# Nine single identity products in two banks instead of four double ones in one, and a new order of all operations

## The chip, the cores and the metric

The kernel runs on one core of a Trainium2 chip. The metric is the time of one execution on the device in microseconds (us), and of several executions the median. The core's engines are TensorE (PE in the profile; its weight loads have a row of their own, PEld), VectorE (DVE), ScalarE (ACT), GpSimd (POOL) and SyncE (SP), which here issues nearly all DMA transfers, in order.

## The reference

There is a linear attention over 8 batches, 8 heads, 576 rows and 64 columns, followed by a feed-forward network (FFN) over the 4608 resulting rows:

```python
q_s = softmax(q, axis=d)          # 64 columns
k_s = softmax(k, axis=s)          # 576 rows
kv  = einsum('bhsd,bhse->bhde', k_s, v)
x   = einsum('bhsd,bhde->bhse', q_s, kv)  -> (4608, 512)
h   = x @ w_in                    # 512 -> 2048
g   = h if h >= 1, 0 if h <= -1, else (h + 1)**2 / 4
out = g @ w_out                   # 2048 -> 512
```

Inputs and outputs are 32-bit floats.

## The kernel before

The 4608 rows are nine chunks of 512 rows. The hidden 2048 columns are sixteen blocks of 128. Each 32-bit operand of the FFN is split into a high and a low part, so that one product of 128x128 by 128x512 is three matmuls (high by low, high by high, low by high).

Chunks 0 to 2 are plain: for each block the first layer (`first_layer`, its matmuls are on line 1496, out is the bank h), then `middle`, which forms g on ACT (relu, line 1666), ACT or POOL (square, lines 1670 and 1672) and DVE (line 1676), then the split of g into its high part on ACT (line 1718) and its low part on DVE (line 1722), then the second layer (line 1733, into four banks o). Chunks 3 to 8 are taken in three pairs, in which two by two blocks of the FFN's matrices are multiplied with seven products instead of eight: the first-layer products are on line 1560 (banks hA, hb, hC), the second-layer ones on line 1876 (banks yA, yB, yC). Weights for these are formed in the plain chunks, stored to device memory (tiles b, s, r) and fetched back as tiles w and w_y (line 650 for the first layer's).

The attention of each chunk runs beside the FFN of an earlier one. The attention of the first chunk stands alone in the head of the program: for each of four head pairs a kt tile (line 996 loads it) has its maximum taken on DVE (nm, line 1013), its exponential on ACT (line 1017), and is transposed on TensorE into the banks ep and et (lines 1024 and 1027); q has its maximum, exponential and sum taken (line 1078), is divided by the sum on POOL (line 1069, with DVE's lines 1082 and 1084 before it) and transposed into tp (line 1089); then kv (line 1042) and x (line 916). In later chunks (`attention_two`) kt is loaded only for its maximum; the maxima go to device memory and come back as a tile m that holds them along the columns (lines 1252 and 1260), k is loaded, has m subtracted on DVE (line 1269) and its exponential taken on ACT (line 1275), and goes into kv (line 1285).

What TensorE does before the first ep is products of the identity matrix with itself, whose results nobody reads. Nine of them (`more_warm`, line 2189) are issued ahead of everything, into the bank o3. `keep_warm` adds operations to the plan that do the same (line 2055); it is called once, for four operations in the bank a.

All operations of all engines are first collected in a list and numbered (`Plan.op`). Then `Plan.settle` puts them in order: SEQUENCE is a written table of all the numbers, and it is the order in which the operations are emitted, and so the order of each engine and of SP's loads and stores; it is asserted that each operation stands behind those that it depends on. SECOND is a table of those operations that go to their second choice of engine. A ring hands out the rooms of a buffer in this order, so the tables also decide which room a tile gets, and which earlier reader it must wait for.

Of the kernel before, what the change touches and what calls it, by code (L numbers as in the profile page):

```python
# [99 lines left out]
class Ring:  # L100
# [330 lines left out]
def tile_linear_attention_then_ffn(  # L431
# [1617 lines left out]
    def keep_warm(pool, tag, n, due):  # L2049

        def again_(i):
            def emit():
                t = pool.tile([P, P], F32, tag=tag, name=f"warm_{tag}_{i}")
                for _ in range(2):
                    nc.tensor.matmul(t, ident, ident, start=True, stop=True)
# [205 lines left out]
```

## Time and profile before

| what | value |
|---|---|
| median of 3 runs | 796.65 us (796.65, 797.94, 794.04) |
| the profiled execution's own time | 800.3 us |
| its span | 798.5 us |
| mean granted TensorE clock | 0.995 |
| PE busy | 783.1 us (98%) |
| DVE, ACT, POOL busy | 591.2, 480.5, 410.8 us |

The span reaches from the first to the last instruction of the core. A matmul's end is modelled in the profile and matmuls are pipelined, so busy time is not time at the peak rate. An idle time is shown in brackets before the instruction that ends it, with the instruction on another engine, or the transfer, that released it.

### The profile page before, as it was taken

The page shows a single profiled execution, that of the slowest core. Times are in us where ns is not written, and L with a number is a line of the kernel's source. Part 1 is how long each engine was busy: PE and PEld are TensorE (multiplying, and loading weights), DVE is VectorE, ACT ScalarE, POOL GpSimd, SP SyncE. Part 2 cuts the span into 40 slices and gives each one's busy share as a digit, 9 for nine tenths or more (in the row PEclk, how much of TensorE's full clock was granted, in tenths as well). Part 3 has the DMA queues.
Part 4 walks back from the last instruction along what each step waited for, and adds up shares of the span by engine and source line. Part 5 has one row for each costly group of instructions (what it writes and reads, how often), then busy time and mean ns, then how long its engine had stood idle before and what let it go on. Part 6 is the DMA issues. An engine that isn't in the chain of part 4 may idle for free.

```text
span 798.5 us, 12268 instructions
## 1 busy us (share of the span) xinstructions
PE 783.1 (98%) x4134; PEld 630.7 (79%) x4134; DVE 591.2 (74%) x996; ACT 480.5 (60%) x895; POOL 410.8 (51%) x355
## 2 busy tenths in 40 slices
PE   7999999999989999999999999999999999999998
PEld 6787888877767778777777888777878888888886
DVE  6988876667757788788878975768897746577942
ACT  6978765544455666565666655676755635556551
POOL 5655676656554645355451564435713444356344
PEclk8999999999999999999999999999999999999999
DMA  8898997989898988888767767666656666666664
GB/s 310 294 294 278 306 340 264 298 269 303 294 316 275 328 279 292 286 288 276 245 192 269 238 234 252 203 222 211 211 184 213 216 205 215 186 206 212 211 210 133
DMA packets 76463, 200.75 MB, mean 251 GB/s; under 512 B 8688, under 2 KB 16880, under 8 KB 76400
## 3 DMA queue, kind: packets, MB, share of 16 engines
q1 hardware_dynamic: 76256, 199.84, 75.4%
q8 instruction: 33, 0.54, 0.3%
q14 instruction: 30, 0.25, 0.1%
q10 hardware_dynamic: 144, 0.13, 0.0%
HBM read 159.02 MB, written 40.91 MB: 250 GB/s over the span
## 4 chain that ended last, share of the span: by engine, by line
PE 75%; DMA 10%; DVE 5%; ACT 3%; POOL 3%; issue 2%; SPq 2%; ACTq 0%; DVEq 0%; POOLq 0%
PE hA L1560 16%; PE yA L1876 16%; PE o L1733 9%; PE hC L1560 8%; PE h L1496 7%; PE yC L1876 7%; PE hb L1560 4%; PE yB L1876 3%; DMA m<-mk 2%; PE x L916 2%; PE kv L1285 1%; DMA mk<-mt 1%; DMA w_y<-r 1%; DMA s<-w_s 1%; DVE k L1269 1%
## 5 line engine op out<-in xcount | busy, mean ns | idle before, releaser
L1852 ACT CAST y<-B 128x512 fp32r<-128x512 f32 x160 | 98.9, 621 | 79.0 <-PE yA L1876 33.1
L1560 PE MATMUL hA<-x,w 128*128 128x512 f32 x576 | 142.2, 391 | 0.9 <-ACT yo L477 0.5
L1856 POOL TENSOR_TENSOR y<-B,y 128x512 fp32r<-128x512 f32 x57 | 79.1, 1390 | 107.2 <-ACT y L1852 107.0
L1560 PEld LDWEIGHTS hA<-x,w 128*128 128x128 f32 x576 | 107.4, 188 | 25.9 <-issue 1.0
L1876 PE MATMUL yA<-y,w_y 128*128 128x512 f32 x528 | 125.1, 390 | 0.0
L1733 PE MATMUL o<-wh,g 128*128 128x512 f32 x384 | 118.7, 390 | 1.7 <-DVE g L1722 1.7
L1876 PEld LDWEIGHTS yA<-y,w_y 128*128 128x128 f32 x528 | 98.8, 188 | 20.7 <-issue 0.2
L1496 PE MATMUL h<-x,w 128*128 128x512 f32 x432 | 109.0, 394 | 4.1 <-DVE g L1722 4.1
L1856 DVE TENSOR_TENSOR y<-B,y 128x512 fp32r<-128x512 f32 x103 | 79.4, 775 | 35.6 <-ACT y L1852 34.8
L1496 PEld LDWEIGHTS h<-x,w 128*128 128x128 f32 x432 | 79.9, 188 | 24.7 <-DVE g L1722 5.5
L1733 PEld LDWEIGHTS o<-wh,g 128*128 128x128 f32 x384 | 72.1, 188 | 17.1 <-DVE g L1722 2.3
L1672 POOL TENSOR_TENSOR r<-r 128x512 f32<-128x512 f32 x45 | 47.2, 1051 | 69.6 <-ACT r L1666 69.6
L1733 PE MATMUL o<-wl,g 128*128 128x512 f32 x192 | 75.7, 394 | 0.0
L1560 PE MATMUL hC<-x,w 128*128 128x512 f32 x288 | 73.1, 390 | 0.0
L1876 PE MATMUL yC<-y,w_y 128*128 128x512 f32 x288 | 66.7, 389 | 0.0
L1670 ACT ACTIVATE r<-r 128x512 f32<-128x512 f32 x99 | 61.9, 631 | 1.8
L1876 PEld LDWEIGHTS yC<-y,w_y 128*128 128x128 f32 x288 | 54.1, 188 | 11.2
L1560 PEld LDWEIGHTS hC<-x,w 128*128 128x128 f32 x288 | 53.8, 188 | 11.4 <-ACT sn_P L477 0.2
L1838 POOL TENSOR_TENSOR B<-B,B 128x512 f32<-128x512 f32 x33 | 47.7, 1453 | 26.1 <-ACT y L1852 9.1
L1393 POOL TENSOR_TENSOR q<-q,qmb 128x512 f32<-128x512 f32 x32 | 37.0, 1169 | 30.8 <-issue 11.4
L1393 POOL TENSOR_TENSOR q<-q,qzb 128x512 f32<-128x512 f32 x32 | 35.8, 1123 | 31.2 <-DVE qzb L1415 18.0
L1838 DVE TENSOR_TENSOR B<-B,B 128x512 f32<-128x512 f32 x63 | 49.4, 797 | 0.8 <-DVE y L1856 0.5
(151 smaller groups left out, 1403.6 us busy)
## 6 DMA issues: line engine op xcount, KB each, us to landing
w_y<-r SPq DMA_DIRECT2D x84, 512.0 KB
w<-b SPq DMA_DIRECT2D x50, 512.0 KB
w<-s SPq DMA_DIRECT2D x48, 512.0 KB
st<-in_w SPq DMA_DIRECT2D x32, 512.0 KB
v<-in_v SPq DMA_DIRECT2D x32, 325.0 KB
q<-in_q SPq DMA_DIRECT2D x36, 256.0 KB
kt<-in_kt SPq DMA_DIRECT2D x32, 288.0 KB
k<-in_k SPq DMA_DIRECT2D x28, 320.0 KB
```

The lines of the kernel that those rows point to most:

```text
L916: nc.tensor.matmul(flat(r)[cols, p0:p1], kvt[rows, g % NKV, pr, :], q[pr]["tq"].rearrange("p j t -> p (j t)")[rows, p0:p1], start=True, st ...
L1269: nc.vector.tensor_tensor(k, k, mb, ALU.subtract)
L1393: nc.gpsimd.tensor_tensor(qf, qf, at, alu)
L1496: nc.tensor.matmul(t["h"], lhs, rhs, start=(turn == 0 and i == 0), stop=(turn == NPAIR - 1 and i == 2),)
L1560: nc.tensor.matmul(banks[b]["h"], lhs, rhs, start=(begins and not kk and not m), stop=(ends and kk == 1 and m == 2), skip_group_check=True,)
L1670: nc.scalar.activation(t["r"], t["r"], AF.Square)
L1672: nc.gpsimd.tensor_tensor(t["r"], t["r"], t["r"], ALU.mult)
L1733: nc.tensor.matmul(outs[c, j], lhs[:, s], rhs, start=(begins and i == 0), stop=(closes and i == 2),)
L1838: eng.tensor_tensor(gr[p, to], gr[p, a], gr[p, b], alu)
L1852: nc.scalar.copy(t["gh"], gr[p, PART_ROOM[part]])
L1856: eng.tensor_tensor(t["gl"], gr[p, PART_ROOM[part]], f32(t["gh"]), ALU.subtract)
L1876: nc.tensor.matmul(banks[b, i], lhs, rhs, start=(begins and not m), stop=(ends and m == 2), skip_group_check=True,)
```

## The change

`keep_warm` issues one product per operation instead of two, and it is called a second time, for five operations in the bank o3. That makes nine single products where there were four double ones. The bank o3 is the one in which the nine products at the start stand.

```diff
@@ keep_warm
         def again_(i):
             def emit():
                 t = pool.tile([P, P], F32, tag=tag, name=f"warm_{tag}_{i}")
-                for _ in range(2):
-                    nc.tensor.matmul(t, ident, ident, start=True, stop=True)
+                nc.tensor.matmul(t, ident, ident, start=True, stop=True)
...
     keep_warm(ps_a, "a", 4, 8.0)
+    keep_warm(ps_o, "o3", 5, 9.0)
...
 SEQUENCE = (
-    86, 1, 11, 12, 13, 19, 22, 87, 0, 3, 88, 89, 4, 23, 20, 30, 31, 32, 14, 43, 46, 47, 15, 16,
...
 SECOND = (
...
```

The two tables are replaced as a whole: SEQUENCE has 3436 numbers instead of 3431 (the five new operations are 90 to 94, and all later numbers are higher by five), SECOND 383 instead of 392. Lines of the changed kernel are one lower than before, and two lower from `keep_warm` on.

On TensorE at the start of the program, ep, et and tp are the transposes of the first attention, with the number of the head pair behind them. Before:

```order
L2189 MATMUL warm<-ident 128x128 x9
L2055 MATMUL warm_a_225<-ident 128x128 x2
L2055 MATMUL warm_a_238<-ident 128x128 x2
L2055 MATMUL warm_a_245<-ident 128x128 x2
L2055 MATMUL warm_a_248<-ident 128x128 x2
L1024 MATMUL ep_0_278<-ident,kt_0_241 128x128 x4
L1027 MATMUL et_0_283<-ident,kt_0_241 128x128
L1024 MATMUL ep_1_286<-ident,kt_1_234 128x128 x4
L1027 MATMUL et_1_291<-ident,kt_1_234 128x128
L1089 MATMUL tp_0_300<-ident,q_0_228 128x128 x4
L1089 MATMUL tp_1_307<-ident,q_1_255 128x128 x4
```

After:

```order
L2053 MATMUL warm_a_269<-ident 128x128
L2053 MATMUL warm_a_283<-ident 128x128
L2053 MATMUL warm_o_0_287<-ident 128x128
L2053 MATMUL warm_o_1_289<-ident 128x128
L2053 MATMUL warm_o_2_291<-ident 128x128
L1088 MATMUL tp_0_299<-ident,q_0_225 128x128 x4
L2053 MATMUL warm_o_3_304<-ident 128x128
L2053 MATMUL warm_o_4_306<-ident 128x128
L1023 MATMUL ep_1_314<-ident,kt_1_242 128x128 x4
L1026 MATMUL et_1_319<-ident,kt_1_242 128x128
L1023 MATMUL ep_0_336<-ident,kt_0_240 128x128 x4
L1026 MATMUL et_0_341<-ident,kt_0_240 128x128
```

The transposes of the first q tile (tp_0) moved ahead of all ep and et, with seven single products ahead of it and two behind it.

On the load queue of SP in the middle of the plain chunks, k tiles are loads of k (the number is the head pair), m the load of the maxima that are subtracted from them (m_3_1 for the head pairs 2 and 3), w and r loads and stores of weights. Before:

```order
L1232 DMA k_0_2532<-in_k 128x640
L799 DMA r_1_170<-wl_112 128x256
L1260 DMA m_4_0_2560<-mk_0_194 128x256
L1232 DMA k_1_2565<-in_k 128x640
L840 DMA r_0_153<-w_o_0_2491 128x512
L840 DMA r_0_157<-w_o_0_2491 128x512
L1252 DMA mk_1_195<-mt_1_2506 4x32 x2
L1232 DMA k_3_2644<-in_k 128x640
L650 DMA w_0_2656<-b_113 128x1024
L799 DMA r_3_172<-wh_1040 128x256
L1260 DMA m_3_1_2659<-mk_1_195 128x256
L1232 DMA k_2_2669<-in_k 128x640
```

After:

```order
L1231 DMA k_2_2410<-in_k 128x640
L1251 DMA mk_0_194<-mt_0_2357 4x32
L1231 DMA k_1_2432<-in_k 128x640
L1231 DMA k_3_2448<-in_k 128x640
L1259 DMA m_4_0_2450<-mk_0_194 128x256
L741 DMA s_1_142<-w_s_1_2318 128x1024
L1231 DMA q_0_2490<-in_q 128x512
L1231 DMA q_1_2498<-in_q 128x512
L1251 DMA mk_1_195<-mt_1_2460 4x32 x2
L1259 DMA m_3_1_2513<-mk_1_195 128x256
L741 DMA s_0_141<-w_s_0_2404 128x1024
L839 DMA r_3_160<-w_o_0_2465 128x512
```

The loads of k_2 and k_3 moved from around the load of m_3_1 to ahead of it by nine and six rows.

On the load queue of SP where the plain chunks end and the first pair begins, w_2_2 is the third of four weight tiles for the third pair of blocks, and kt_0 and kt_1 are loads for the attention of a later chunk. Before:

```order
L650 DMA w_3_0_3863<-b_119 128x1024
L650 DMA w_2_1_3914<-s_0_133 128x1024
L1232 DMA kt_1_3916<-in_kt 128x576
L650 DMA w_1_3_3918<-b_116 128x512
L650 DMA w_2_2_3961<-s_1_134 128x1024
L650 DMA w_2_3_3963<-b_118 128x512
L1232 DMA q_2_3977<-in_q 128x512
```

After:

```order
L649 DMA w_2_1_3945<-s_0_133 128x1024
L1251 DMA mk_1_199<-mt_1_3736 4x32 x2
L2027 DMA out<-osb_0_3873 128x512
L1231 DMA kt_0_3976<-in_kt 128x576
L649 DMA w_2_2_3988<-s_1_134 128x1024
L649 DMA w_3_1_3996<-s_0_135 128x1024
L1259 DMA m_5_1_3998<-mk_1_199 128x256
L649 DMA w_3_0_4011<-b_119 128x1024
L649 DMA w_2_3_4013<-b_118 128x512
```

The load of kt_0 stands right ahead of w_2_2 now; before, kt_1 stood two rows ahead of it.

On TensorE around the use of the same tile, before:

```order
L1285 MATMUL kv_0_3889<-v_1_3617,k_1_3614 64x65 x10
L1560 MATMUL hC_1_3833<-x_2946,w_1_2_3817 128x512 x3
L1560 MATMUL hC_1_3833<-x_3540,w_1_2_3817 128x512 x3
L1560 MATMUL hb_2_3926<-x_3066,w_2_0_3739 128x512 x3
L1560 MATMUL hb_2_3926<-x_3453,w_2_0_3739 128x512 x3
L1560 MATMUL hA_2_3869<-x_3345,w_2_1_3914 128x512 x3
L1560 MATMUL hA_2_3869<-x_3456,w_2_1_3914 128x512 x3
L1560 MATMUL hC_2_3948<-x_3646,w_2_1_3914 128x512 x3
L1560 MATMUL hC_2_3948<-x_3650,w_2_1_3914 128x512 x3
L1560 MATMUL hA_1_3751<-x_3601,w_1_3_3918 128x512 x3
L1560 MATMUL hA_1_3751<-x_3722,w_1_3_3918 128x512 x3
L1560 MATMUL hA_2_3869<-x_3641,w_2_2_3961 128x512 x3
```

After:

```order
L1284 MATMUL kv_0_3917<-v_0_3489,k_0_3710 64x65 x10
L1284 MATMUL kv_0_3917<-v_1_3915,k_1_3617 64x65 x10
L1559 MATMUL hA_2_3897<-x_3540,w_2_1_3945 128x512 x3
L1559 MATMUL hA_2_3897<-x_3551,w_2_1_3945 128x512 x3
L1559 MATMUL hb_2_3965<-x_3059,w_2_0_3871 128x512 x3
L1559 MATMUL hb_2_3965<-x_3335,w_2_0_3871 128x512 x3
L1559 MATMUL hC_2_3979<-x_3688,w_2_1_3945 128x512 x3
L1559 MATMUL hC_2_3979<-x_3727,w_2_1_3945 128x512 x3
L1559 MATMUL hA_2_3897<-x_3697,w_2_2_3988 128x512 x3
```

Between the kv multiplication and the first product with w_2_2 there are three groups of six matmuls now, and five before.

## Rows read from the trace of the kernel before

**Rows 1.** The page: the busy time of each engine with its share of the span and its instructions, and the chain of work that ended last, by engine.

```profile
PE 783.1 (98%) x4134; PEld 630.7 (79%) x4134; DVE 591.2 (74%) x996; ACT 480.5 (60%) x895; POOL 410.8 (51%) x355
...
PE 75%; DMA 10%; DVE 5%; ACT 3%; POOL 3%; issue 2%; SPq 2%; ACTq 0%; DVEq 0%; POOLq 0%
```

**Rows 2.** The table of stretches over the whole span. Columns: stretch and its length, then busy time with the number of instructions of PE, PEld, DVE, ACT and POOL, the granted TensorE clock as a share of full speed, the share of the DMA engines, GB/s.

```profile
0.00:35.10 35.10, 30.67 (x214) 23.86 (x214) 28.03 (x61) 27.62 (x57) 21.62 (x25) 0.90 0.85 294
35.10:150.00 114.90, 114.86 (x624) 92.42 (x625) 91.77 (x163) 82.75 (x155) 72.68 (x66) 1.00 0.89 300
150.00:350.00 200.00, 193.81 (x1154) 154.17 (x1156) 149.36 (x280) 111.54 (x223) 105.52 (x102) 1.00 0.88 293
350.00:550.00 200.00, 198.98 (x1061) 159.64 (x1053) 154.31 (x257) 125.53 (x236) 98.11 (x80) 1.00 0.72 238
550.00:798.50 248.50, 244.74 (x1093) 200.62 (x1091) 167.68 (x239) 133.05 (x228) 112.88 (x85) 1.00 0.62 200
```

**Rows 3.** What TensorE's matmuls waited for over the whole span: total us, number of waits, the longest.

```profile
PE h L1496 <- DVE g L1722: 4.1, 4, 2.6
PE tp L1089 <- POOL q L1069: 2.6, 2, 1.8
PE o L1733 <- DVE g L1722: 1.7, 1, 1.7
...
PE hA L1560 <- DMA w<-s: 0.3, 1, 0.3
```

**Rows 4.** TensorE's matmuls in order of time from the start to 36 us: start, length, then line, operation, tiles and count; in brackets the idle time just before and who ended it.

```profile
5.36 2.92 PE L2055 MATMUL warm_a<-ident 128*128 128x128 f32 x16
8.12 0.60 PE L1024 MATMUL ep<-ident,kt 128*128 128x128 f32 x4
...
11.18 0.66 PE L1089 MATMUL tp<-ident,q 128*128 128x128 f32 x4 [1.78 <-POOL q L1069]
12.63 1.12 PE L1089 MATMUL tp<-ident,q 128*128 128x128 f32 x4 [0.80 <-POOL q L1069]
...
14.96 1.11 PE L1024 MATMUL ep<-ident,kt 128*128 128x128 f32 x4
...
16.22 1.35 PE L1042 MATMUL kv<-v,k 128*64 128x65 f32 x20
...
21.20 0.80 PE L1042 MATMUL kv<-v,k 128*64 128x65 f32 x20
...
35.15 3.02 PE L1496 MATMUL h<-x,w 128*128 128x512 f32 x12 [0.35 <-DVE g L1722]
```

**Rows 5.** TensorE's weight loads in order of time, the first two groups of the identity products; columns as in rows 4.

```profile
5.16 0.62 PEld L2055 LDWEIGHTS warm_a<-ident 128*128 128x128 f32 x4
6.03 0.52 PEld L2055 LDWEIGHTS warm_a<-ident 128*128 128x128 f32 x4 [0.25 <-PE warm_a L2055]
```

**Rows 6.** The table of stretches at the start of the program; columns as in rows 2.

```profile
11.50:12.00 0.50, 0.33 (x4) 0.09 (x1) 0.50 (x2) 0.35 (x3) 0.47 (x1) 1.00 1.05 409
...
13.00:19.00 6.00, 6.00 (x58) 4.77 (x58) 5.27 (x17) 5.24 (x12) 4.99 (x5) 0.50 0.99 393
...
19.20:20.00 0.80, 0.80 (x20) 0.53 (x20) 0.76 (x4) 0.55 (x4) 0.39 (x2) 1.00 0.23 82
```

**Rows 7.** All engines in order of time around 9 us, the rows of VectorE and GpSimd; columns as in rows 4.

```profile
8.87 0.75 DVE L1013 TENSOR_REDUCE nm<-kt 128x1 f32<-128x576 f32 x1 [0.77 <-DMA kt<-in_kt]
...
9.73 0.20 DVE L1084 RECIPROCAL qrz<-qz 128x8 f32<-128x8 f32 x1
...
10.08 1.04 POOL L1069 TENSOR_TENSOR q<-q,qrz 128x512 f32<-128x512 f32 x1 [1.45 <-DVE qrz L1084]
```

**Rows 8.** What ScalarE waited for between 17 and 23 us; columns as in rows 3.

```profile
ACT k L477 <- PE ep L1024: 0.7, 1, 0.7
ACT kvt L892 <- PE kv L1042: 0.2, 1, 0.2
ACT tb L477 <- PE tp L1089: 0.2, 1, 0.2
ACT x L931 <- PE x L916: 0.2, 1, 0.2
```

**Rows 9.** TensorE's matmuls that begin after the longest idle times between 180 and 270 us, in order of time (columns as in rows 4), and below the dots one piece of the chain of waits back from 233 us: start, length, what.

```profile
180.79 0.50 PE L1733 MATMUL o<-wh,g 128*128 128x512 f32 x1 [1.68 <-DVE g L1722]
...
228.45 3.02 PE L1496 MATMUL h<-x,w 128*128 128x512 f32 x12 [2.56 <-DVE g L1722]
...
266.75 0.93 PE L1496 MATMUL h<-x,w 128*128 128x512 f32 x3 [0.88 <-DVE g L1722]
...
219.31 5.90 DMA k<-in_k
```

**Rows 10.** First what the load queue on SP waited for between 300 and 345 us (columns as in rows 3), then pieces of three chains of waits, from 315 to 350, from 400 to 425 and from 490 to 505 us (columns as in the last row of rows 9).

```profile
SPq L1232 <- PE kv L1285: 6.4, 1, 6.4
...
315.27 1.36 PE hA L1560 x6
...
326.86 5.56 DMA w<-s
...
412.94 7.38 DMA w_y<-r
...
496.24 3.50 DMA w<-b
```

484 rows, old and new, of tables (SECOND, SEQUENCE) are left out of this document.

## Prediction

> **What bounds the kernel now.** I read the page first. TensorE (PE) is busy 783.1 of 798.5 us and carries 75% of the chain that ended last [rows 1]; no other engine passes 74%. The instruction count on it grows by one 128x128 product while the matrix work stays the same, so the change can take off no more than the time in which TensorE stands idle, or runs at the lower clock. Next came the table of stretches [rows 2], to find where that time is: 4.43 us are idle before 35.10, 0.04 from there to 150, 6.19 between 150 and 350, 1.02 between 350 and 550, and 3.76 after 550, nearly all of it the last copy and store, since the last product ends near 794.8. The clock is below full in one stretch only, the first. The list of waits [rows 3] names who is waited for: transposes tp wait for the q tiles of GpSimd (2.6 us), first-layer products for the low part of g (4.1), second-layer products for the same (1.7), the rest are loads of 0.3 to 0.4.
>
> The head was read in TensorE's timeline [rows 4] beside the windows with the clock [rows 6]. In rows 6 the granted clock is still 1.00 up to 12.00, though TensorE is idle for 1.78 us before 11.18 and 0.80 before 12.63 [rows 4]; then it is 0.50, the lower level of 1.2 GHz, through 13 to 19 (the transposes of 12.63, 1.12 us where those of 11.18 took 0.66, show it first), and 1.00 again from 19.20. At half clock the twenty kv products of 16.22 take 1.35 us, those of 21.20 at full clock 0.80 [rows 4]. So two idle gaps came before the fall, and the fall costs more than the gaps.
>
> **The change part by part.**
>
> *The head.* Before, the four double identity products end where ep begins, at 8.1, and ep_0/et_0/ep_1/et_1 fill 8.12 to 9.40 (11.18 less 1.78). Then comes nothing but tp_0 (0.66) until tp_1 at 12.63. Now seven single products stand first. A double one takes 0.77 us from start to start, 0.25 of it a wait of its weight load for the product before in the same bank [rows 5], so a single one takes 0.26 to 0.51, and four in one bank and three in the other about 3.1 to 3.3, from 5.16 to 8.3 or 8.5. Then tp_0, which waits for q_0 divided by its row sums: in the new order DVE no longer does the maximum of a kt tile (0.75 us, and 0.77 of waiting for its load) ahead of that row's two small steps [rows 7], so the GpSimd product, 1.04 us, starts near 8.4 instead of 10.08, and tp_0 near 9.5 instead of 11.18. Two more single products follow (to about 10.8 if they wait for tp_0, which they stand behind), then ep_1, et_1, ep_0, et_0 (1.28 us for both pairs, from 8.12 to 9.40), then tp_1, whose q_1 still ends at about 12.6 on GpSimd. TensorE's idle time between 8.4 and 12.6 is then some 1.1 + 0.8 us, against 1.78 + 0.80, and the two gaps have work of 2.3 us between them and not 0.66.
>
> If the clock holds, the work of 12.63 to 19.05, 6.4 us at half clock, needs about 3.2. Not all of that can come out: ACT feeds the same stretch (exponentials, copies of ep, tp, the weight parts) and waits for TensorE only 0.7 + 0.2 + 0.2 + 0.2 us between 17 and 23 [rows 8]. So the gain is at most 1.3; on the other side the clock may fall before ep and et, and then a pair of them takes 1.26 us (14.96 to 16.22) instead of 0.64 (half of 1.28) [rows 4]: 1.2 lost on the two. I take 0.65 of 1.2, that is -0.8: in rows 6 the clock outlived one idle microsecond and a half with only 0.66 of work in between, and the new row has less idle time at the same place. The next thing that is late there is the first product of the fifth block, which at 35.15 waits for g of the third [rows 4]; the DVE work before it is the same in both orders, and that caps the gain too.
>
> The Trainium skill speaks against this part: "TensorE: Matmul & The Clock Gate", section "A second HAM failure mode: psum-queue depth-cycling", says that short idle spells between groups of products, as a kernel cycles through its banks, can make the clock go up and down though each product looks normal. Nine single products in two banks are such groups. The trace so far disagrees in the mild case: doubles with 0.25 us between them from 5.36 to 8.12 kept 1.00 in the windows of rows 6 behind them. By that rule the head would lose the 1.2 us instead of winning 0.8.
>
> *The middle.* Of the 6.19 us, three waits make most: 1.68 at 180.79, 2.56 at 228.45 and 0.88 at 266.75 [rows 9]. The chain of waits back from 228.45 is g, h, and a subtraction on DVE (k minus its maximum) that stood 5.90 us for the load of its k tile [rows 9]: DVE was stopped by an operation that served attention, and the FFN operation behind it was late. Before, that load is issued right behind the load of the maximum tile m, among the last of its group; now both k tiles of that head pair are issued six to nine places ahead of m, and the subtractions stand 14 and 19 places behind the transposed maximum on DVE. The 2.56 and the rest of its kind behind it (4.1 in all for four waits, [rows 3]) were led by that stop; I count the 2.56 and 0.3 as gone. In the same way the k loads of the next unit move from both sides of its m tile to ahead of it. What remains is the reason why a g operation can be late at all: one bank per block, and this is as before. Other operations that wait on loads now stand elsewhere, so I cannot say that 1.68 and 0.88 go; a wait like them may also come at a new place. Ends: -6.2 (all gone) to +3 (one more wait as long as the 2.56). I take half of 6.19, -3.1, near the 2.56 whose cause moved.
>
> *The transition from plain chunks to pairs.* The load queue on SP is in order, and a load that waits for room holds all behind it: between 300 and 345 one load on it waited 6.4 us for kv products [rows 10]. In the new order a kt load that needs the room which a kv multiplication frees stands right ahead of four weight loads of 512 KB. On TensorE only three groups of six products are then between kv and the first product with the weights of the next load: 18 x 0.2267 us (1.36 for six, [rows 10]) = 4.08 us. The same kind of load ended 5.56 us after its issue where TensorE waited for it (from 326.86), with 3.50 and 7.38 as the ends that the trace shows for such tiles [rows 10]. So the wait is 0 to 3.3, and I take 5.56 - 4.08 = +1.5. Two later first products of a pair also have shorter cover (about 4.1 to 4.8 us): +0.5 for both. The old wait there was 0.3 [rows 3], and I leave it, as the small ones behind it.
>
> *Engines.* Some forty operations change engine: conversions from ACT to DVE, stores' copies from DVE to ACT, sums from DVE to GpSimd and lows back. The busy sums hardly change, and each has TensorE work beside it with 26% to 49% of the engine free; 0. Without that cover one of them, late, would cost its own time, like the 0.75 us of the DVE row in rows 7. The tail ends with the same chain of products, copy and store: 0.
>
> **Sum.** -0.8 - 3.1 + 1.5 + 0.5 = -1.9 us on the profiled execution's 800.3, so 798.4. That execution lies 3.65 above the median of the runs shown, 796.65, so 794.7 as a median.
>
> **Rivals.**
> - *All gaps close.* The k loads were the only cause, the first loads of pairs stay covered, the clock holds: -6.2 - 1.3 = -7.5, 789.2. For it: every long wait of the middle is one of g on DVE. Against: 180.79 has another cause upstream (a weight load and its conversion), which I could not follow into the new order.
> - *The load queue.* The kt load behind the kv multiplication holds the weights of three products in turn: 3.3 at the first, then 0.5 and 1.0 where cover is 4.8 and 4.1, and no gain in the middle since a new late load stops DVE there: +4.8, 801.4, slower. It decides from a landing over 5.6 us. For it: the 6.4 us already stood in the queue. Against: that same 6.4 cost TensorE only 0.3 [rows 3].
> - *The clock falls earlier*, by the idle time between singles, with the middle and transition as forecast: +1.2 in place of -0.8, so 2.0 above the forecast, 796.7.
> - *Nothing happens*: the waits move but do not shrink and the head is bound by ACT and DVE: 796.6.
>
> **How the numbers follow.** Forecast 0.42, all gaps close 0.25, load queue 0.15, clock 0.08, nothing 0.10. About 0.5% (4.0 us) is what a measurement tells from no change: 792.7 to 800.6. The forecast's own range is 791.5 to 797.5, from its halved middle term; with a third of it under 792.7 and nearly all of the first rival, faster gets 0.36; of the load queue two thirds and a little of the rest lie above 800.6, so slower gets 0.13, and 0.51 is left for same. The range reaches from 789 into the first rival to 800 on the other side, where about two in ten are left out.
>
> **What would show it.** In the windows, clock 1.00 from 12 to 19 (kv groups of 0.80 us) or 0.50; tp_0 near 9.5. In the waits, h on g below 2 us in all, no DVE subtraction that stands long for in_k. hA waiting for a weight load 1 to 2 us near 325 to 335, right behind a kv group. Wrong if TensorE's idle time between 150 and 350 stays at 6 or above, if a loss appears after 350 where I expect almost none, or if the half-clock stretch gets longer.

## The result and the profile after

The changed kernel takes 800.61 us as the median of 20 runs (795.43 to 807.84), against 796.47 us for 20 runs of the kernel before. The ratio of the time after to the time before is 1.0054, with a 95% interval of 1.0034 to 1.0074: it is slower by 4 us, where 2 us less were forecast. Beside each other on another chip the ratio was 1.0064.

Its runs scatter more than those of the kernel before, and they go with the clock: the runs at a mean granted clock of 0.999 or 1.000 took 795.4 to 801.1 us, those at 0.997 or below 802.9 to 807.8, and those at 0.998 lie across both (799.0 to 804.0). The profiled execution is one of the former, 798.06 us with a span of 796.3. It is *shorter* than the profiled execution of before (800.3), although the medians say the opposite. That is the first thing to read here: neither of the two profiles is an ordinary execution.

The table of stretches, answering to [rows 2], with the columns told there:

```profile
0.00:35.10 35.10, 31.30 (x223) 23.66 (x224) 28.38 (x63) 27.84 (x57) 22.77 (x26) 1.00 0.89 309
35.10:150.00 114.90, 113.44 (x618) 90.80 (x617) 92.77 (x164) 78.89 (x151) 67.75 (x60) 1.00 0.87 297
150.00:350.00 200.00, 195.12 (x1159) 153.98 (x1158) 140.89 (x259) 115.03 (x228) 123.06 (x115) 1.00 0.86 294
350.00:550.00 200.00, 200.00 (x1061) 161.62 (x1060) 163.53 (x270) 126.57 (x235) 101.11 (x84) 1.00 0.71 237
550.00:796.30 246.30, 242.51 (x1083) 198.95 (x1081) 164.85 (x239) 134.00 (x229) 98.84 (x75) 1.00 0.63 201
```

Idle time of TensorE: 3.80 us in the head (4.43 before), 1.46 from 35 to 150 (0.04), 4.88 from 150 to 350 (6.19), none from 350 to 550 (1.02), 3.79 in the rest (3.76). The clock is 1.00 throughout. What it waited for, answering to [rows 3]:

```profile
PE h L1495 <- DMA w<-b: 2.4, 3, 1.2
PE hA L1559 <- DMA w<-b: 1.7, 1, 1.7
...
PE tp L1088 <- POOL q L1068: 1.3, 2, 0.8
...
PE hA L1559 <- DMA w<-s: 0.5, 1, 0.5
...
PE o L1732 <- DVE g L1721: 0.2, 1, 0.2
```

The waits for g, 4.1 + 1.7 us, have shrunk to 0.2 in this execution. In their place TensorE waits for weights that are fetched back from device memory, w: 2.4 + 1.7 + 0.5 us. The head, answering to [rows 4], and the clock there, to [rows 6]:

```profile
5.32 2.02 PE L2053 MATMUL warm_a<-ident 128*128 128x128 f32 x8
7.18 1.48 PE L2053 MATMUL warm_o<-ident 128*128 128x128 f32 x6
9.49 0.66 PE L1088 MATMUL tp<-ident,q 128*128 128x128 f32 x4 [0.83 <-POOL q L1068]
9.99 0.93 PE L2053 MATMUL warm_o<-ident 128*128 128x128 f32 x4
...
12.11 0.66 PE L1088 MATMUL tp<-ident,q 128*128 128x128 f32 x4
...
13.70 1.53 PE L1041 MATMUL kv<-v,k 128*64 128x65 f32 x40
```

```profile
11.50:12.00 0.50, 0.50 (x5) 0.27 (x3) 0.47 (x3) 0.50 (x2) 0.50 (x1) 1.00 1.06 317
13.00:19.00 6.00, 5.29 (x77) 3.13 (x76) 4.83 (x17) 5.38 (x13) 4.79 (x4) 1.00 0.97 374
```

Each identity product has two records, so x8, x6 and x4 are four, three and two of them. tp_0 starts at 9.49 instead of 11.18, and the kv products of 13.70 take 1.53 us for forty; those of 16.22 in [rows 4] took 1.35 for twenty. The nine products are where the change put them, and the clock does not fall.

How much the head gained is not told by its idle time, which products that nobody reads can fill: `warm_a` and `warm_o` are busy for 3.9 us here and `warm_a` for 2.7 before. It is told by the first product of the FFN, which stands behind the first attention. Before, and then after:

```profile
22.37 0.94 PE L1496 MATMUL h<-x,w 128*128 128x512 f32 x3
```

```profile
21.34 0.96 PE L1495 MATMUL h<-x,w 128*128 128x512 f32 x3
```

That is one microsecond earlier than in the one profile of before that the prediction had.

### The profile page after: what moved, and what is told of

The parts are those of the page before. It is cut to its first block, busy times and chain, and to the rows that moved or that the text cites. A ratio compares the mean times of both kernels' runs of the same rounds, so it can differ in the third digit from the quotient of the medians.

```text
span 796.3 us, 12311 instructions
## 1 busy us (share of the span) xinstructions
PE 782.4 (98%) x4136; PEld 629.0 (79%) x4136; DVE 590.4 (74%) x990; ACT 482.3 (61%) x897; POOL 413.5 (52%) x359
## 4 chain that ended last, share of the span: by engine, by line
PE 80%; DMA 8%; DVE 5%; ACT 3%; issue 2%; POOL 1%; SPq 1%; POOLq 0%; ACTq 0%; DVEq 0%
PE yA L1875 16%; PE hA L1559 16%; PE h L1495 10%; PE o L1732 10%; PE yC L1875 8%; PE hC L1559 7%; PE yB L1875 4%; PE hb L1559 4%; DMA w<-b 4%; PE kv L1284 2%; PE x L915 2%; DMA kt<-in_kt 1%; DMA s<-w_s 1%; ACT r L1665 1%; DMA r<-w_o 1%
## 5 line engine op out<-in xcount | busy, mean ns | idle before, releaser
L1855 DVE TENSOR_TENSOR y<-B,y 128x512 fp32r<-128x512 f32 x104 | 83.1, 806 | 27.4 <-ACT y L1851 27.1
L1671 POOL TENSOR_TENSOR r<-r 128x512 f32<-128x512 f32 x41 | 44.2, 1078 | 74.3 <-ACT r L1665 73.9
L1669 ACT ACTIVATE r<-r 128x512 f32<-128x512 f32 x103 | 64.9, 632 | 2.6
L1837 POOL TENSOR_TENSOR B<-B,B 128x512 f32<-128x512 f32 x31 | 41.8, 1358 | 28.3 <-DVE B L1675 13.6
L1837 DVE TENSOR_TENSOR B<-B,B 128x512 f32<-128x512 f32 x65 | 47.6, 745 | 1.1 <-POOL y L1855 0.6
L1392 POOL TENSOR_TENSOR q<-q,qmb 128x512 f32<-128x512 f32 x32 | 34.9, 1105 | 23.9 <-DVE qmb L1384 19.2
L1665 ACT ACTIVATE r<-h,half 128x512 f32<-128x512 f32 x48 | 33.0, 687 | 21.5 <-PE h L1495 20.1
```

What stands on the lines that cost most here:

```text
L1392: nc.gpsimd.tensor_tensor(qf, qf, at, alu)
L1665: nc.scalar.activation(t["r"], t["h"], AF.Relu, bias=half[:, :1], scale=0.5)
L1669: nc.scalar.activation(t["r"], t["r"], AF.Square)
L1671: nc.gpsimd.tensor_tensor(t["r"], t["r"], t["r"], ALU.mult)
L1837: eng.tensor_tensor(gr[p, to], gr[p, a], gr[p, b], alu)
L1855: eng.tensor_tensor(t["gl"], gr[p, PART_ROOM[part]], f32(t["gh"]), ALU.subtract)
```

## The experiments

Theory A after the result: the loss comes from stored weights that land late, held up on the load queue, and the head is a small gain. Rivals: B, the single products make the clock fall in most executions; C, the loss lies after 381 us; D, the slower executions are slow for a cause that no profile had shown.

**Which part of the order.** Three kernels take a part of the order table and of the engine table from each kernel; nothing is left out of the computation in any kernel here. Every ratio below is to the kernel before on the same chip.

```diff
 e1_new_head     SEQUENCE = first 306 of the new, then the rest as in the old
 e2_old_head     SEQUENCE = first 301 of the old (four double products), then the rest as in the new
 e3_new_to_381   SEQUENCE = first 2058 of the new, then the rest as in the old
```

> The first 306 operations (to about 44 us) in the new order with the nine single products, all later ones in the old order. Theory A (the loss comes from stored weight tiles w that land late between 80 and 350 us, and the head is a small gain): 1 to 2 us under the kernel before, no waits of TensorE for w of 1 us or more. Rival B (the single products let the clock fall in most executions, and the head is the loss): 3 to 5 us over the kernel before, a granted clock of 0.50 for some us before 40.

> The first 301 operations in the old order with the four double products, all later ones in the new order. Theory A: 5 to 6 us over the kernel before, with waits for w near 89, 253, 266 and 346 as in the changed kernel. Rival B: within 1 us of the kernel before.

> The first 2058 operations (to about 381 us) in the new order, all later ones in the old order. Theory A: 3 to 5 us over the kernel before, as the changed kernel. Rival C (the loss lies in the pairs after 381 us, where the one profile of the changed kernel shows no idle time but slower executions may): within 1 us of the kernel before, or under it.

> The changed kernel as it is, for its time beside the others on one chip and for a second profile. Theory A: 3 to 5 us over the kernel before; if the profiled execution is one of the slower ones, the waits for w are longer than in the first profile (5.8 us in all there), and no wait of 1 us or more has another cause. Rival B: the granted clock falls in the first 40 us in a slower execution. Rival C: idle time after 381 us.

Measured on one chip: e2 1.0057 (1.0037 to 1.0076), e3 1.0082 (1.0054 to 1.0110), e4 1.0064 (1.0036 to 1.0091), and e1 1.0161. With the old head the loss is the same as with the new one, so B falls; with the old order behind 381 us it is there too, so C falls. e3 lies above both expectations: 0.0082 is some 6.5 us, where 3 to 5 were expected. e1 missed both as well. In it the seam, the place where one order ends and the other begins, is what is measured; its two longest waits are in neither kernel:

```profile
66.17 0.50 PE L1719 MATMUL o<-wl,g 128*128 128x512 f32 x1 [4.42 <-POOL wl L598]
...
112.36 0.76 PE L1719 MATMUL o<-wl,g 128*128 128x512 f32 x1 [3.45 <-ACT g L1704]
```

(columns as in [rows 4]; both lie behind the seam at 44 us, in chunk 0, whose weights were begun in the one order and ended in the other). It says nothing on the head but this: to 35 us it had the new head's clock of 1.00.

**The nine products alone.** The old order and engines, with the new products where the old ones stood:

```diff
 SEQUENCE (old order), on TensorE:
-warm_a x2, warm_a x2, warm_a x2, warm_a x2, ep_0, ...
+warm_a, warm_a, warm_a, warm_a, warm_o, warm_o, warm_o, warm_o, warm_o, ep_0, ...
```

> The order and the engines of the kernel before, with nine single products (four in bank a, five in o3) where the four double ones stood. Theory A (the identity products change little, the loss is the load queue): within 1 us of the kernel before. Rival B (singles in two banks let the clock fall, or delay the first transposes): 2 us or more over it, with a granted clock of 0.50 from an earlier time than in the kernel before.

795.51 us against 796.48, ratio 0.9982 (0.9958 to 1.0005). The part of the change that its words name costs nothing that can be measured, and may win a microsecond.

**The load queue.** These are the rows of the place that the prediction named, in the changed kernel: SP's transfers in order of time (start, time of issue, line, transfer, count), then what the queue waited for between 310 and 360 us (columns as in [rows 3]), one piece of the chain of waits back from 346 us, and TensorE's matmuls that waited there.

```profile
336.68 0.34 SPq L1231 DMA_DIRECT2D kt<-in_kt  x1
337.07 0.90 SPq L649 DMA_DIRECT2D w<-s  x2
338.13 0.32 SPq L1259 DMA_DIRECT2D m<-mk  x1
338.50 1.42 SPq L649 DMA_DIRECT2D w<-b  x2
```

```profile
SPq L1231 <- PE kv L1284: 8.2, 2, 4.4
...
338.50 7.53 DMA w<-b
```

```profile
341.41 1.63 PE L1559 MATMUL hA<-x,w 128*128 128x512 f32 x6 [0.48 <-DMA w<-s]
...
346.07 1.65 PE L1559 MATMUL hA<-x,w 128*128 128x512 f32 x6 [1.66 <-DMA w<-b]
```

The kt load waited 4.4 us on the queue and is issued at 336.68, right after the kv multiplication whose room it takes. The two weight loads behind it (w<-s) follow at 337.07, the next two (w<-b) at 338.50, and products that need such weights begin at 341.41 and 346.07 after 0.48 and 1.66 us of waiting; the load that ends the second wait took 7.53 us from its issue. The edits take this apart, and with it a second place near 260 us, where a load whose room came free late stood ahead of one whose product came sooner:

```diff
 e9_kt_alone: SP's order near 337 us
-kt_0, w_2_2, w_3_1, m_5_1, w_3_0, w_2_3, w_3_2
+w_2_2, w_3_1, m_5_1, w_3_0, w_2_3, w_3_2, kt_0
 e10_swap_alone: SP's order near 260 us, each load keeps its room
-w_9, w_10
+w_10, w_9
 e6_loads_ahead = e9 + e10
 e11_more_swaps = e6, and
-w_7, ..., w_6 / w_13, w_11
+w_6, ..., w_7 / w_11, w_13
```

> The changed kernel with two moves on the load queue alone: the load of kt_0, which waits for a kv multiplication, goes behind the five weight loads that it held up near 337 us, and of two weight loads near 260 us the one whose product comes first is issued first, each keeping its room. Theory A: the waits of hA for w of about 2.1 us near 341 and 346 and the wait of h for w of 1.2 to 1.6 us near 266 go, so 2 to 4 us under the changed kernel on the same chip. Rival D (what makes the changed kernel slow in most executions is another thing, a stretch at the lower clock whose place no profile has shown yet): under 1 us.

> The changed kernel with the load of kt_0 behind the five weight loads, and nothing else. Theory A1 (the kt load that waits for the kv multiplication is the main loss, 2.1 us in the faster executions and more in the slower ones): within 1 us of the version with both moves, 4 us or more under the changed kernel; no wait of hA for w over 0.5 us; the 1.2 to 1.9 us wait of h for w near 266 stays. Rival A2 (the two weight loads near 260 us are the larger part): 2 us or less under the changed kernel.

> The changed kernel with the two weight loads near 260 us exchanged, and nothing else. Theory A1: 1 to 2 us under the changed kernel, still 2 to 4 over the kernel before, with hA waiting about 2.1 us for w near 346. Rival A2: within 1 us of the version with both moves.

> Both moves, and two more pairs of weight loads exchanged so that the one whose product comes first is issued first (near 237 us and one behind 262 us), each keeping its room. If the order on the load queue is all that is left of h waiting for w (2.2 us in the profile of the version with both moves): 0.5 to 1.5 us under that version, 2 to 3 under the kernel before. If the loads are late because the rooms are free late: no change.

| kernel | median | ratio to before | interval |
|---|---|---|---|
| changed kernel (e4) | 800.05 | 1.0064 | 1.0036 to 1.0091 |
| e10, exchange near 260 alone | 798.97 | 1.0047 | 1.0024 to 1.0069 |
| e9, kt load behind alone | 796.52 | 1.0015 | 1.0001 to 1.0030 |
| e6, both | 795.12 | 0.9982 | 0.9961 to 1.0003 |
| e11, both and two more pairs | 793.50 | 0.9975 | 0.9955 to 0.9995 |

The runs of the table are of three chips (e4; e6; e9 to e11), so ratios are compared, not medians. One transfer moved by six places takes about 0.004 to 0.005 of the ratio away, 3 to 4 us of the 4 to 5 lost (between e10 and e6, 0.0065). The exchange near 260 alone is worth 0.7 to 1.7 thousandths, within the intervals. Both together, e6, take away more than the 2 to 4 us that were expected, and can no longer be told from the kernel before; e11 lies just under that kernel, and can't be told from e6. e9 did not come "within 1 us" of e6 (0.0033 of the ratio lie between them), so the second place is not nothing. What TensorE waited for in e9, and then in e10 (their lines are 14 and 8 lower than the changed kernel's):

```profile
PE h L1481 <- DMA w<-b: 4.8, 3, 2.5
...
PE hA L1545 <- DMA w<-b: 0.4, 1, 0.4
```

```profile
PE h L1487 <- DMA w<-b: 2.2, 2, 1.4
...
PE hA L1551 <- DMA w<-b: 1.2, 1, 1.2
...
PE hA L1551 <- DMA w<-s: 0.6, 1, 0.6
```

In e9 the wait of hA is gone but for 0.4, and that of h is there (4.8 in this execution); in e10 hA still waits 1.2 + 0.6, and h waits twice instead of three times (as it does in two of the later profiles of the changed kernel). In e11 no wait for w is left. The stretches of [rows 2] between 150 and 350, cut at 300, first in the changed kernel and then in e11:

```profile
150.00:300.00 150.00, 147.34 (x909) 116.26 (x908) 103.96 (x194) 88.39 (x176) 95.39 (x89) 1.00 0.86 296
300.00:350.00 50.00, 47.77 (x252) 37.72 (x251) 36.93 (x66) 26.64 (x52) 27.67 (x27) 1.00 0.86 288
```

```profile
150.00:300.00 150.00, 148.82 (x917) 118.19 (x916) 105.70 (x197) 89.32 (x177) 100.50 (x92) 1.00 0.88 302
300.00:350.00 50.00, 49.97 (x264) 40.07 (x263) 39.13 (x68) 30.27 (x58) 25.50 (x25) 1.00 0.89 300
```

That is 2.66 and 2.23 us of idle time in the one, 1.18 and 0.03 in the other. Of the 36 runs of e6, e9 and e11 the slowest took 799.17; of the 20 of the changed kernel 14 took more than that.

**What an ordinary execution of before looks like.** The same kernel, for two more profiles:

> The kernel before as it is, for a second profile. If the losses counted in the prediction are ordinary: about 7 us at 0.50 in the first 20 us, and about 5 us of TensorE waiting for g between 150 and 270. If the first profile was an unusual execution: 3 us or less at 0.50, and 1 to 3 us less waiting for g, at a time near 796.

> The kernel before once more, for a third profile: about 7 us at 0.50 and 5 us of waiting for g if the first profile was ordinary, 3 us or less at 0.50 and 2 to 4 us of waiting if it was not.

They took 794.98 and 796.43 us. The stretches from 12 to 20 and from 150 to 300, and the first product of the FFN, e13 and then e14:

```profile
12.00:20.00 8.00, 6.95 (x106) 4.81 (x106) 7.35 (x24) 7.43 (x18) 5.99 (x6) 1.00 0.93 348
150.00:300.00 150.00, 147.48 (x908) 116.35 (x908) 111.50 (x211) 83.32 (x166) 87.41 (x83) 1.00 0.88 298
...
20.08 0.96 PE L1496 MATMUL h<-x,w 128*128 128x512 f32 x3
```

```profile
12.00:20.00 8.00, 7.49 (x92) 5.49 (x94) 7.19 (x23) 7.58 (x18) 6.47 (x6) 0.79 0.86 335
150.00:300.00 150.00, 147.33 (x910) 116.70 (x909) 111.23 (x213) 83.85 (x167) 85.30 (x83) 1.00 0.88 299
...
20.99 0.94 PE L1496 MATMUL h<-x,w 128*128 128x512 f32 x3
```

From 150 to 300 TensorE is idle for 2.52 and 2.67 us; in the first profile it was 5.9 (6.19 less the 0.28 behind 300). In the head e13 never falls below full clock, and e14 has 0.79 over 8 us, some 3.4 us at half clock where the first profile had about 7. The first product of the FFN, at 22.37 in the first profile, begins at 20.08 and 20.99 here; in the six profiles of the changed kernel that can be used it begins at 20.72 to 21.34. The losses that the prediction set out to win back were mostly those of one unusual execution. They do come back now and then: e5, in the old order and at 798.45 the slowest of its twelve runs, has one wait for g of 2.79 us and 3.60 us of idle time from 150 to 300.

**The slower executions of after.**

> The changed kernel as it is, for a profile of another execution. Its runs so far fall in two groups, near 798 us at a mean granted clock of 1.0 and near 804 at 0.995; both profiles so far are of the first. Theory A: a slower execution has longer waits for w at the known places. Rival D: it has a stretch of 6 to 8 us at 0.50, in the head, and the waits for w are as long as in the others.

> The same kernel once more, with the same expectations: one of the two should be a slower execution.

> The changed kernel once more for a profile, in the hope of an execution of the slower group (near 804 us). Theory A: longer waits for w at the known places, above all near 346, and if one is long enough a stretch at the lower clock behind it. Rival D: a stretch at 0.50 in the head.

> The changed kernel for another profile. Near 798: as the others, 2.0 us or so of hA waiting for w at 340 to 347. Near 804, by theory A: 4 us or more there and a stretch at the lower clock behind it; by rival D: a stretch at 0.50 in the head, and about 2 us at 340 to 347.

> The changed kernel once more: near 798 with about 2 us of hA waiting for w at 340 to 347, or near 804 with either 4 us or more there (theory A) or a stretch at 0.50 in the head (rival D).

e7 was an execution of 4471.35 us and is not used: TensorE alone was slow in it (busy 4464 us, a product of 128x512 took 1.70 us instead of 0.39), at a granted clock that the profile gives as 1.00, while the other engines' busy times are within 5% of those in the first profile. e8, e12 and e15 took 799.03, 798.67 and 798.76, e16 803.73. hA's wait at 345 to 352 is there in all four: 2.04, 1.51, 2.23 and 1.72 us. In e15 one can see what may follow it, in TensorE's row and the windows around it:

```profile
344.85 2.72 PE L1559 MATMUL hA<-x,w 128*128 128x512 f32 x6 [2.23 <-DMA w<-b]
```

```profile
342.00:344.80 2.80, 0.62 (x3) 0.19 (x1) 1.27 (x2) 0.00 (x0) 0.00 (x0) 1.00 0.98 393
344.80:346.00 1.20, 1.15 (x3) 0.96 (x4) 1.20 (x3) 0.00 (x0) 0.00 (x0) 0.63 1.03 408
346.00:348.00 2.00, 2.00 (x8) 0.97 (x10) 2.00 (x4) 0.39 (x1) 1.17 (x1) 0.50 0.70 269
348.00:350.00 2.00, 2.00 (x20) 1.25 (x13) 1.63 (x3) 0.93 (x2) 0.11 (x1) 0.87 0.68 196
```

The idle time ends at 344.8, and the mean clock is 0.63 to 346, 0.50 to 348 and 0.87 to 350; between the two levels of 0.50 and 1.00 that is 0.9 + 2.0 + 0.5, some 3.4 us at half clock. The six products take 2.72 us instead of the 1.65 of 346.07. In e16 the same happened at another place, 91 us. TensorE's row, VectorE's two rows ahead of it, and the windows:

```profile
91.22 2.44 PE L1284 MATMUL kv<-v,k 128*64 128x65 f32 x40 [2.50 <-DMA w<-b]
```

```profile
86.04 3.23 DVE L1268 TENSOR_TENSOR k<-k,m 128x640 f32<-128x640 f32 x2 [2.34 <-DMA m<-mk]
...
90.31 0.69 DVE L584 SCALAR_TENSOR_TENSOR st<-sg,st 128x512 uint32<-128x512 uint32 x1
```

```profile
91.00:92.00 1.00, 0.78 (x15) 0.81 (x16) 0.93 (x5) 0.00 (x0) 0.15 (x1) 0.59 1.04 426
92.00:94.00 2.00, 2.00 (x32) 1.88 (x30) 1.46 (x4) 1.17 (x2) 1.27 (x2) 0.50 0.75 236
```

The profile puts this wait down to a weight load, but kv reads no weight. It needs the bank a, which the join of line 584 has to read first; that ends at 91.00, 0.22 us ahead of kv, as it does in the first profile of after (88.94 and 89.16); VectorE was late because its subtractions of line 1268 had waited 2.34 us for the maxima and then took 3.23 us (1.56 and 1.55 in e8 and e12). The mean clock is 0.59 and 0.50 up to 94, so forty kv products take 2.44 us, where those of 335.25 in the first profile took 1.39. So D has it half right: part of the excess of e16 is a stretch at the lower clock, but it is not in the head, it stands behind a wait. e16 was not shown to be typical: it is one execution, and its place, 91 us, lies ahead of everything that e6 and e9 changed. Nor is a low clock all there is to slow executions: four of the six runs of e3 have a mean clock of 1.000 and took 799.2 to 803.9 us. On e4's chip both kernels have the same mean clock over their runs, 0.998. The runs at 1.000 took 797.6 us after and 794.9 before (medians of 6 and 3), those at 0.997 or below 804.3 and 796.7 (5 each): the changed kernel loses some 3 us without a low clock, and more with it.

## Why the prediction was wrong

**What each stretch costs.** Idle time leaves out the clock, the identity products and a little at each wait, since a product is drawn to 0.39 us in the profile though the next one starts 0.23 us behind it. So count the work instead: every matmul at the usual distance to the next one of its form in these traces, the identity products at nothing. What is left of a stretch is lost. It is an estimate from the traces, in which only differences between kernels count; us lost, means of the profiles named:

| stretch (us) | first of before | e13, e14 | first of after, e4, e8, e12, e15 | e16 |
|---|---|---|---|---|
| 0 to 35.1 | 15.0 | 13.2 | 13.3 | 13.2 |
| 35.1 to 150 | 1.9 | 2.9 | 2.5 | 7.4 |
| 150 to 300 | 12.4 | 9.1 | 10.2 | 11.3 |
| 300 to 350 | 0.9 | 0.7 | 4.2 | 1.8 |
| 350 to 550 | 5.6 | 5.2 | 3.6 | 5.3 |
| 550 to the end | 4.7 | 4.7 | 4.7 | 4.9 |

**The middle** is the step that failed: "I take half of 6.19, -3.1, near the 2.56 whose cause moved." Two things were wrong in it. The 6.19 were measured in an execution 3.65 us above its median, and in e13 and e14 the idle time there is 2.5 and 2.7 us, the wait of 2.56 at 228.45 only 1.41 and 0.68; the text noted the distance to the median and then subtracted the whole of the losses as though they belonged to every execution. And the gaps did not close: 150 to 300 has 2.66, 3.95, 3.52, 4.43, 3.16 and 4.21 us in the six profiles of after (first, e4, e8, e12, e15, e16). The waits for g went as forecast, to between 0 and 1.0 us. With the k loads ahead of m, no subtraction waits for its k any more (5.9, 4.0 and 4.2 us in the three profiles of before), though the waits for m mostly grew (9 to 13 us in all before, 12 to 20 after); that moving these loads alone does it was not tried. Loads of w near 243, 253 and 266 took their place, each held up by a load ahead of it or by a store whose room it takes. "A wait like them may also come at a new place" stood in the prediction as an end of the range, and was the ordinary case. The term was about +1.1, not -3.1. The prediction's own sign of being wrong, 6 us or more idle between 150 and 350, is not there in the first profile (4.88) and is there in e4, e8 and e12 (6.25, 6.52 and 6.59).

**The transition** was right in mechanism and place, and too small. Predicted were +2.0 us from the kt load behind the kv multiplication. As idle time that fits: from 300 to 350 the profiles of after have 2.23 (first), 2.30 (e4), 3.00 (e8), 2.16 (e12) and 2.52 us (e15) (in e16 it lies behind 350), and those of before 0.28, 0 and 0. But it fits in part by luck: +1.5 was meant for the first product with the late weights and +0.5 for later ones, and it is the first that waits 0.5 us or less and a later one that waits 1.5 to 2.2. As lost time it is 3.5 us, which agrees with the 3 to 4 that undoing that one order wins; in four of the five the clock is 1.00 throughout, and e15, with half clock behind the wait, lost 5.5 where they lost 3.7 to 4.3. The rival of the load queue was nearest, with its 801.4 against 800.61, and had a chance of 0.15; its account of the middle, a late load that stops VectorE, is not what the traces show.

**The head** came out as worked in its times: tp_0 at 9.49 where 9.5 was expected, full clock from 12 to 19. Its gain of 0.8 was not there. The first product of the FFN begins at 21.1 on average, against 20.08 and 20.99 in e13 and e14, and with the old head the loss is the same (e2 beside e4: 1.0057 and 1.0064). The fall of the clock that was to be won back is a property of the execution too: in e13 four double products kept full clock. The rule of the Trainium skill weighed there ("TensorE: Matmul & The Clock Gate", section "A second HAM failure mode: psum-queue depth-cycling") is not borne out for the single products: the windows at 11.50 and 13.00 show 1.00 behind them. The stretches at the lower clock that profiles of the changed kernel show stand behind waits of over 2 us in dense work.

**After 350** nothing was expected and about 1.5 us was won: to 550 nothing is idle in five profiles of after (1.53 us in e16), against 1.02, 0.41 and 1.99 in those of before. What in the order does it was not looked for. **Engines and tail** were right at 0.

Put together, against e13 and e14: +0.1 in the head, -0.4 to 150, +1.1 in the middle, +3.5 at the transition and -1.5 behind it are +2.8 us, where -1.9 was forecast, and these five executions of after are 2.7 us longer than those two. The five lie 2.2 us under the median of the changed kernel, the two 0.8 under that of the kernel before; these 1.4 us make up the measured 4.1. They lie in the slower executions of the changed kernel. e15 and e16 show one thing that is in them, a stretch at half clock behind one of the waits; how much of the 1.4 is of that kind stays open.

## What to carry to other kernels

A sum over the gaps of one profile takes that execution's bad luck for a property of the kernel: before a wait is counted as a gain, ask whether the profiled execution is near the median, and look at a second profile if it is not. When an order is replaced as a whole, go through the load queue for each load that waits for room, list what stands behind it, and compare the time to the first use; one load moved by six places there (e9) was worth more than all that the new order won elsewhere. A short wait in dense TensorE work is priced by what the clock does after it, too.

## What was not expected of the hardware

A wait of 2.23 us between dense products (e15), one of 2.50 (e16) and, in the old order, one of 2.79 (e5) were followed by some 3.4 us at half clock, while waits of 2.04 (e8), 2.47 (e3), 2.48 (e9) and 2.56 us (228.45 in the first profile of before) were followed by full clock: a wait may or may not cost nearly twice its length. And the same two subtractions on VectorE near 84 us took 1.55 or 1.56 us together in four profiles of the changed kernel, 2.68 in its first and 3.23 in e16, where they began late. In these two GpSimd was at work beside them (on lines 611 and 1671); in the four it was not, or only for part of one of them. Over the 17 usable traces, 239 such subtractions had nothing on GpSimd beside them and took 0.78 to 0.83 us each, and all 121 that took more than 0.90 had. No experiment moved the work of GpSimd away.
